# Three chained blocks on one core: the remainders of a float64 MoE moved from GpSimd to VectorE, and the second MoE's gathers, block order and scatters changed

## The chip, the cores and the metric

The kernel runs on one core of a Trainium2 chip. The metric is the device time of one execution in microseconds (us). The core has five engines with queues of their own: TensorE (PE in the profile; PEld is its weight load), VectorE (DVE), ScalarE (ACT), GpSimd (POOL) and SyncE (SP), which here only starts DMA transfers. Each engine runs its instructions in order; one that waits holds up all behind it on that engine.

## The reference, cut to what matters

```python
# attention: 4 batches, 12 heads, 448 rows, 64 wide; causal
scores = scale * q @ k^T;  scores = where(mask, -1e9, scores)
x = softmax(scores) @ v            # -> 1792 tokens x 768
# first MoE: every token through the same two matrices (float64 inputs)
h = x @ w_in                       # 768 -> 2048
x = (h - tanh(h)) @ w_out          # 2048 -> 768
# second MoE: one of 8 experts per token
logits = x @ w_gate + modality_bias[modality_id]
e = argmax(logits);  gate = softmax(logits)[e]
out[token] = gate * (relu(x[token] @ w1[e]) @ w2[e])   # 768 -> 1024 -> 768
```

`w_in` and `w_out` come as float64; the rest is float32.

## The kernel before

**Products in two parts.** Each float32 operand of a MoE product is split in two: `hi` is the value rounded to TensorE's fp32r format by a copy, and `lo` is the remainder, value minus `hi` (`split_lo`, line 69). A product is then three matmuls: hi x hi, hi x lo, lo x hi. `split_lo` takes the engine as an argument, and the copy before it has an engine of its own, so each split is a hand-over between two engines, or two instructions on one.

**Attention and the first MoE.** The tokens go in four batches of 448. While attention works on batch b+1 (six pairs of heads per batch, `attn_tick`), the first MoE works on batch b (`moe_steps`): 16 pieces of `w_in` in layer 1 (`l1`), 16 of `w_out` in layer 2 (`l2`), each piece 128 x 768. `take` hands out the MoE's steps between the attention's, in proportion to costs written in the list. `split_piece(n + 2)` is called as piece n is begun, so a piece is prepared two ahead; there are two buffers for `w_raw` and `w_lo` and three for `w_hi`. For batch 0 a piece is loaded as float64 words (`w_wide`, two buffers) and `narrow` (line 363) makes float32 of it: one conversion on ScalarE (L368), three integer instructions on VectorE (L372, L376, L380), and a DMA that keeps the narrowed piece in memory for batches 1 to 3. Then ScalarE copies `w_hi`, and GpSimd computes `w_lo` (line 396). GpSimd also computes `x_lo`, the remainder of attention's output, for all batches (line 406), and `g_lo`, the remainder between the two layers, for batch 0 (line 433); in later batches `g_lo` is on VectorE.

The softmax of batches 0 and 1 is left undivided, and the division is spread by small products (`ps_rc`, L273); in batches 2 and 3 VectorE divides.

**The second MoE.** Tokens are sorted by expert into blocks of 256 (`up_wide`) and one half block of 128 (`up_half`). The first two blocks (`first`) are of the expert that has most tokens after three batches, and are chosen before the fourth is through. `more()` routes the rest while block 0 runs, and returns five wide blocks, then the half block. A block needs 14 weight pieces: 6 of `w1` (128 x 1024) and 8 of `w2` (128 x 768), each fetched by an indirect DMA that GpSimd issues (`gather_w`), copied to `e_hi` on ScalarE and subtracted to `e_lo` on VectorE (`split_w`, line 910). There are four raw buffers (`e_raw`), and a gather is issued five pieces ahead of the one in work, a split two ahead. The first four gathers are issued while the first MoE still runs; splits 0 and 1 then go to a pool of their own (`e0`), and the pools `h` and `e` open only when the first MoE's memory is given back (`moe_ctx.close()`). Each block's rows are gathered by `gather_x` in the block before, and its results are scattered to `out` by an indirect DMA from GpSimd for each 128 rows (line 1090). All scatters write the same tensor, so each is ordered behind the one before.

**What sets the order.** The framework that the kernel is written in places the waits and buffers and sets each engine's order when the kernel is built, from the order of the program and its own modelled times; it may put an instruction that is ready before one that is not.

Of the kernel before, what the change touches and what calls it, by code (L numbers as in the profile page):

```python
# [8 lines left out]
F32 = mybir.dt.float32  # L9
# [8 lines left out]
P = 128  # L18
# [16 lines left out]
def kernel(  # L35
# [14 lines left out]
    nc = tc.nc  # L50
# [12 lines left out]
    def copy(eng, out, in_):  # L63
        if eng is nc.scalar:
            eng.activation(out=out, in_=in_, func=AF.Copy)  # L65
        else:
            eng.tensor_copy(out=out, in_=in_)

    def split_lo(eng, lo, full, hi):
        eng.tensor_tensor(out=lo, in0=full, in1=hi.bitcast(F32), op=ALU.subtract)  # L70
# [185 lines left out]
    def emit_pv(p):  # L256
# [26 lines left out]
        if b == 0:  # L283
            split_x(p)
        else:
            x_done.add(p)
# [31 lines left out]
    xhi, xlo = {}, {}  # L318
    pieces, raw_w = {}, {}
    NPC = 2 * KF  # L320
    order = [(b, j) for b in range(B) for j in range(NPC)]
# [3 lines left out]
    wide = w_in.dtype != F32  # L325
# [61 lines left out]
    def split_piece(n):  # L387
        if n >= len(order):
            return
        raw = raw_w.pop(n)  # L390
        if wide and order[n][0] == 0:
            raw = narrow(n, raw)
        hi = mp.tile([P, KD, P], F32R, tag="w_hi", name="w_hi", bufs=3)
        lo = mp.tile([P, KD, P], F32R, tag="w_lo", name="w_lo", bufs=2)
        copy(nc.scalar, hi, raw)
        split_lo(nc.gpsimd, lo, raw, hi)
        pieces[n] = (hi, lo)
        load_piece(n + 2)

    def split_x(p):  # L400
        b, hp = divmod(p, NP)
        xhi[b, hp] = mp.tile([P, S], F32R, tag=f"x_hi{hp}", name="x_hi")
        xlo[b, hp] = mp.tile([P, S], F32R, tag=f"x_lo{hp}", name="x_lo")
        t = x32.pop(p)
        copy(nc.scalar if b else nc.vector, xhi[b, hp], t)
        split_lo(nc.gpsimd, xlo[b, hp], t, xhi[b, hp])

    def moe_steps(b):
        base = b * NPC
        g_hi, g_lo = [], []  # L410
        cur = {}

        def l1(f, s):
            if s == 0:
                split_piece(base + f + 2)
                cur["ps"] = ps_m.tile([P, 512], F32, tag="m", name="ps_h")
            ps = cur["ps"][:, 0:S]
            whi, wlo = pieces[base + f]
            for kk in (2 * s, 2 * s + 1):
                for n, (a, x) in enumerate(((whi, xhi), (whi, xlo), (wlo, xhi))):  # L420
                    nc.tensor.matmul(  # L421
                        ps, a[:, kk, :], x[b, kk],
                        start=(kk == 0 and n == 0), stop=(kk == KD - 1 and n == 2),
                    )
            if s == 2:
                pieces.pop(base + f)
                t = mp.tile([P, S], F32, tag="tmp", name="tanh", bufs=2)
                nc.scalar.activation(out=t, in_=ps, func=AF.Tanh)  # L428
                nc.vector.tensor_tensor(out=t, in0=ps, in1=t, op=ALU.subtract)  # L429
                g_hi.append(mp.tile([P, S], F32R, tag=f"g_hi{f}", name="g_hi"))  # L430
                g_lo.append(mp.tile([P, S], F32R, tag=f"g_lo{f}", name="g_lo"))
                copy(nc.scalar if b == 0 else nc.vector, g_hi[f], t)
                split_lo(nc.gpsimd if b == 0 else nc.vector, g_lo[f], t, g_hi[f])

        def l2(j, s):
            if s == 0:
# [87 lines left out]
    pool2 = {}  # L524
    BT = 256
    NFIRST = 2
    NSTAT = NT // BT - NFIRST
    NBLK = (NT - 1 - (NT - S + E - 1) // E) // BT + E + 1
    FE = w1.shape[2]
# [64 lines left out]
    def ps_route(nm):  # L594
        if "r" in pool2:
            return pool2["r"].tile([P, 512], F32, tag="r", name=nm)
        return ps_t.tile([P, 512], F32, tag="t", name=nm)
# [288 lines left out]


    NT2 = BT // P
    G_AHEAD = 5
    w1r = w1.rearrange("e d f -> (e d) f")  # L890
    w2r = w2.rearrange("e f d -> (e f) d")

    def off(ap):
        return bass.IndirectOffsetOnAxis(ap=ap, axis=0)

    def gather_w(blk, i):
        t = pool2["w"].tile([P, FE], F32, tag="e_raw", name="e_raw", bufs=4)
        if i < KD:
            nc.gpsimd.indirect_dma_start(  # L899
                out=t, out_offset=None, in_=w1r, in_offset=off(blk["w1"][i]),  # L900
                bounds_check=E * DM - 1, oob_is_err=False,
            )
        else:
            nc.gpsimd.indirect_dma_start(
                out=t[:, 0:DM], out_offset=None, in_=w2r, in_offset=off(blk["w2"][i - KD]),
                bounds_check=E * FE - 1, oob_is_err=False,
            )
        blk["raw", i] = t
# [111 lines left out]
    def moe2(blocks, more=None):  # L1020
        seq = [(b, i) for b in blocks for i in range(KD + KE)]

        def ahead(n, f):
            if n < len(seq):
                f(*seq[n])

        if "xt" not in blocks[0]:
            gather_x(blocks[0])
            for n in range(G_AHEAD):
                ahead(n, gather_w)  # L1030
            for n in range(2):
                ahead(n, split_w)
            turn_x(blocks[0])
        else:
            ahead(G_AHEAD - 1, gather_w)
        for u, blk in enumerate(blocks):
            nxt = blocks[u + 1] if u + 1 < len(blocks) else None
            n0 = u * (KD + KE)
            nt = len(blk["g"])

            def step(i, n0=n0, nxt=nxt):
                ahead(n0 + i + 2, split_w)
                ahead(n0 + i + G_AHEAD, gather_w)
                if i == 2 and nxt is not None:
                    gather_x(nxt)

            hid = (up_wide if nt == NT2 else up_half)(blk, step)
            nch = DM // BT
            po = [
                pool2["l2"].tile([P, 2, BT], F32, tag=f"l2_{n}", name="ps_l2")  # L1050
                for n in range((nt * nch + 1) // 2)
            ]
            for f in range(KE):
                step(KD + f)
                whi, wlo = blk.pop(("w", KD + f))
                th, tl = hid[f]
                for t in range(nt):
                    ts_ = slice(t * P, (t + 1) * P)
                    for m, (a, w) in enumerate(((th, whi), (th, wlo), (tl, whi))):
                        for h in range(nch):  # L1060
                            c = t * nch + h
                            nc.tensor.matmul(  # L1062
                                po[c // 2][:, c % 2, :], a[:, ts_], w[:, h * BT:(h + 1) * BT],
                                start=(f == 0 and m == 0 and c % 2 == 0),
                                stop=(
                                    f == KE - 1 and m == 2
                                    and (c % 2 == 1 or c == nt * nch - 1)
                                ),
                            )
                if f == KE - 1 and u == 0 and more is not None:  # L1070
                    new = more()
                    blocks.extend(new)
                    seq.extend((b, i) for b in new for i in range(KD + KE))
                if f == KE - 3 and nxt is not None:
                    turn_x(nxt)
            for t in range(nt):
                ob = pool2["h"].tile([P, DM], F32, tag="ob", name="ob", bufs=4)
                gt = blk["x"][t][:, DM:DM + 1]
                h = 0
                while h < nch:  # L1080
                    c = t * nch + h
                    n = 2 if c % 2 == 0 and h + 1 < nch else 1
                    o = ob[:, h * BT:(h + n) * BT]
                    src = po[c // 2][:, c % 2:c % 2 + n, :].rearrange("p a b -> p (a b)")
                    if n == 2:
                        nc.scalar.activation(out=o, in_=src, func=AF.Copy, scale=gt)
                    else:
                        nc.vector.tensor_scalar_mul(o, src, gt)
                    h += n
                nc.gpsimd.indirect_dma_start(  # L1090
                    out=out, out_offset=off(blk["s"][t]), in_=ob, in_offset=None,
                    bounds_check=NT - 1, oob_is_err=False,
                )

    def clear_last():
        z = mp.tile([P, 768], F32, tag="w_raw", name="zrow", bufs=2)
# [8 lines left out]
    def run():  # L1105
# [66 lines left out]
            take(state["used"] + 0.1)  # L1172
        first = route_first(ps_route("ps_a"))
        gather_x(first[0])
        for i in range(4):
            gather_w(first[0], i)
        while len(state["fill"]) > 12:
            take(state["used"] + 0.1)
# [13 lines left out]
        routed = {}  # L1192

        def more():
            half, routed["rest"], routed["tot"] = route_rest(ps_route("ps_b"))
            return routed["rest"][:NSTAT] + [half]

        moe2(first, more)
        rest, tot = routed["rest"], routed["tot"]
        n = nc.values_load(tot[0:1, 0:1], min_val=0, max_val=NBLK)  # L1200
# [37 lines left out]
```

## Time and profile before

| | |
|---|---|
| three runs | 1057.69, 1058.78, 1059.7 us (median 1058.78) |
| profiled execution | 1053.05 us |
| its span, first to last instruction | 1051.3 us |
| mean granted clock of TensorE | 0.981 |
| TensorE busy, 0 to 89 us (attention of batch 0) | 79.7 |
| TensorE busy, 464 to 630 us (batch 2 of the first MoE) | 165.7 |
| TensorE busy, 630 to 766 us (batch 3, without attention beside it) | 131.2 |
| TensorE busy, 766 to 1051.3 us (second MoE) | 267.0 |

The profile is that of one execution. Its rows give an engine, a line of the kernel, output and inputs by name, how often, how long, and what ended the idle time before. The granted clock is the share of full speed that TensorE was given. Names are those of the program without buffer numbers.

### The profile page before, as it was taken

The page shows a single profiled execution, that of the slowest core. Times are in us where ns is not written, and L with a number is a line of the kernel's source. Part 1 is how long each engine was busy: PE and PEld are TensorE (multiplying, and loading weights), DVE is VectorE, ACT ScalarE, POOL GpSimd, SP SyncE. Part 2 cuts the span into 40 slices and gives each one's busy share as a digit, 9 for nine tenths or more (in the row PEclk, how much of TensorE's full clock was granted, in tenths as well). Part 3 has the DMA queues.
Part 4 walks back from the last instruction along what each step waited for, and adds up shares of the span by engine and source line. Part 5 has one row for each costly group of instructions (what it writes and reads, how often), then busy time and mean ns, then how long its engine had stood idle before and what let it go on. Part 6 is the DMA issues. An engine that isn't in the chain of part 4 may idle for free.

```text
span 1051.3 us, 17253 instructions
## 1 busy us (share of the span) xinstructions
PE 995.7 (95%) x6366; PEld 847.3 (81%) x6366; DVE 625.9 (60%) x1333; ACT 513.2 (49%) x1061; POOL 457.9 (44%) x326
## 2 busy tenths in 40 slices
PE   6999889698999999999999998999989999999994
PEld 3667667577777888878878887999889999999994
DVE  4867888757665663455674429641376645655563
ACT  4766556555554554444455433432234544554553
POOL 0215455333333443433353346554255465546552
PEclk9999999899999999999999999999989999999997
DMA  7744667676534344343323236343246676676763
GB/s 158 194 120 117 194 192 218 195 206 205 148 93 145 105 111 118 101 116 102 102 85 93 84 113 189 113 140 116 72 152 212 212 226 224 199 233 220 226 198 116
DMA packets 141564, 162.02 MB, mean 154 GB/s; under 512 B 77215, under 2 KB 112543, under 8 KB 141472
## 3 DMA queue, kind: packets, MB, share of 16 engines
q1 hardware_dynamic: 127040, 99.03, 33.5%
q0 software_dynamic: 14432, 61.81, 18.8%
q8 instruction: 52, 0.85, 0.3%
q14 instruction: 40, 0.33, 0.1%
HBM read 135.77 MB, written 25.43 MB: 153 GB/s over the span
## 4 chain that ended last, share of the span: by engine, by line
PE 67%; issue 9%; DVE 8%; POOL 6%; DMA 5%; ACT 4%; SPq 0%; POOLq 0%; ACTq 0%; DVEq 0%
PE ps_x L445 19%; PE ps_h L421 16%; PE ps_l L1062 8%; PE ps_sc L185 5%; PE ps_l L969 5%; PE ps_xt L262 4%; PE ps_pt L242 4%; DVE w_raw L376 2%; DVE w_raw L380 2%; POOL w_lo L70 2%; DMA e_raw<-in_moe_w_dram,a_i 2%; DMA e_raw<-in_moe_w_dram,b_i 1%; PE ps_tr L145 1%; ACT w_raw L368 1%; POOL e_raw L899 1%
## 5 line engine op out<-in xcount | busy, mean ns | idle before, releaser
L70 POOL TENSOR_TENSOR w_lo<-w_raw,w_hi 128x768 fp32r<-128x768 f32 x128 | 247.6, 1935 | 307.8 <-PE ps_x L445 124.3
L65 ACT ACTIVATE w_hi<-w_raw 128x768 fp32r<-128x768 f32 x128 | 107.9, 844 | 180.3 <-DMA w_raw<-w 115.9
L70 DVE TENSOR_TENSOR e_lo<-e_raw,e_hi 128x768 fp32r<-128x768 f32 (+1 forms) x112 | 119.7, 1072 | 111.3 <-ACT e_hi L916 110.8
L916 ACT ACTIVATE e_hi<-e_raw 128x768 fp32r<-128x768 f32 (+1 forms) x112 | 104.8, 939 | 137.6 <-PE ps_l L1062 59.6
L421 PE MATMUL ps_h<-x_hi,w_hi 128*128 128x448 f32 x384 | 151.9, 396 | 10.2 <-DVE tanh L429 10.1
L445 PE MATMUL ps_x<-g_hi,w_hi 128*128 128x448 f32 x384 | 150.8, 393 | 0.0
L421 PE MATMUL ps_h<-x_lo,w_hi 128*128 128x448 f32 x384 | 142.2, 370 | 1.2 <-POOL x_lo L70 1.2
L445 PE MATMUL ps_x<-g_hi,w_lo 128*128 128x448 f32 x384 | 141.7, 369 | 1.2 <-POOL w_lo L70 1.2
L421 PE MATMUL ps_h<-x_hi,w_lo 128*128 128x448 f32 x384 | 142.0, 370 | 0.5 <-POOL w_lo L70 0.5
L445 PE MATMUL ps_x<-g_lo,w_hi 128*128 128x448 f32 x384 | 141.8, 369 | 0.0
L211 ACT ACTIVATE s_sb<-s_sb,mx 112x112 f32<-112x112 f32 (+1 forms) x192 | 99.6, 521 | 76.5 <-DVE mx L195 76.1
L195 DVE CUSTOM_DVE_ANT_0 s_sb<-ps_sc,mask 112x112 f32<-112x112 f32 (+1 forms) x192 | 77.1, 443 | 67.2 <-PE ps_sc L185 66.5
L421 PEld LDWEIGHTS ps_h<-x_hi,w_hi 128*128 128x128 f32 x384 | 72.9, 190 | 31.0 <-DVE tanh L429 13.1
L969 PE MATMUL ps_l<-xt_hi,e_lo 128*128 128x256 f32 x336 | 94.4, 281 | 0.0
L969 PE MATMUL ps_l<-xt_hi,e_hi 128*128 128x256 f32 x336 | 94.1, 280 | 0.0
L969 PE MATMUL ps_l<-xt_lo,e_hi 128*128 128x256 f32 x336 | 93.6, 279 | 0.0
L445 PEld LDWEIGHTS ps_x<-g_hi,w_hi 128*128 128x128 f32 x384 | 73.2, 190 | 13.5 <-issue 7.9
L445 PEld LDWEIGHTS ps_x<-g_hi,w_lo 128*128 128x128 f32 x384 | 73.1, 190 | 7.9 <-POOL w_lo L70 1.9
L421 PEld LDWEIGHTS ps_h<-x_hi,w_lo 128*128 128x128 f32 x384 | 73.0, 190 | 6.9 <-POOL w_lo L70 0.9
L421 PEld LDWEIGHTS ps_h<-x_lo,w_hi 128*128 128x128 f32 x384 | 73.3, 191 | 6.1 <-POOL x_lo L70 1.8
L445 PEld LDWEIGHTS ps_x<-g_lo,w_hi 128*128 128x128 f32 x384 | 73.5, 191 | 4.4
L429 DVE TENSOR_TENSOR tanh<-ps_h,tanh 128x448 f32<-128x448 f32 x64 | 39.6, 619 | 60.2 <-ACT tanh L428 60.1
(216 smaller groups left out, 1934.5 us busy)
## 6 DMA issues: line engine op xcount, KB each, us to landing
w_raw<-w SPq DMA_DIRECT2D x96, 384.0 KB, 3.1
w_wide<-in_moe_w_in_dram SPq DMA_DIRECT2D x16, 768.0 KB, 5.6
w<-w_raw SPq DMA_DIRECT2D x32, 384.0 KB, 2.8
w_wide<-in_moe_w_out_dram SPq DMA_DIRECT2D x12, 768.0 KB, 4.9
qr<-in_q_dram SPq DMA_DIRECT2D x48, 112.0 KB, 3.2
kr<-in_k_dram SPq DMA_DIRECT2D x48, 112.0 KB, 3.2
vr<-in_v_dram SPq DMA_DIRECT2D x48, 112.0 KB, 3.2
x2s<-tok SPq DMA_DIRECT2D x24, 224.0 KB, 3.3
```

The source lines that it names most:

```text
L65: eng.activation(out=out, in_=in_, func=AF.Copy)
L70: eng.tensor_tensor(out=lo, in0=full, in1=hi.bitcast(F32), op=ALU.subtract)
L185: nc.tensor.matmul(ps[:CP, x, o:o + w], qT[r, c * CP:(c + 1) * CP], kT[r, 0:w], start=(o == 0), stop=(c == S_GROUPS[g][-1]),)
L195: nc.vector.tensor_tensor_reduce(out=d["s"][c], in0=ps[:CP, x, at[c]:at[c] + w], in1=mask[:, S - w:S], scale=1.0, scalar=3.0e38, op0=ALU.a ...
L211: nc.scalar.activation(out=s, in_=s, func=AF.Exp, scale=-1.0, bias=d["mx"][c], accum_out=sums[p][:, x, c:c + 1],)
L242: nc.tensor.transpose(ps[:CP, o + (c - kc) * CP:o + (c - kc + 1) * CP], d["s"][c][:, kc * CP:(kc + 1) * CP], ident[:CP, :CP],)
L262: nc.tensor.matmul(ps[64 * x:64 * x + 64, kc * CP:S], vt[:, kc, x, :], st[2 * p + x]["pt"][kc], start=(kc == 0), stop=(kc == NC - 1),)
L421: nc.tensor.matmul(ps, a[:, kk, :], x[b, kk], start=(kk == 0 and n == 0), stop=(kk == KD - 1 and n == 2),)
L445: nc.tensor.matmul(ps, a[:, r, :], x[f], start=(f == 0 and n == 0), stop=(f == KF - 1 and n == 2),)
L916: nc.scalar.activation(out=hi[:, 0:n], in_=raw[:, 0:n], func=AF.Copy)
L969: nc.tensor.matmul(o, a[:, fs], x, start=(kk == 0 and m == 0 and f % 2 == 0), stop=(kk == KD - 1 and m == 2 and f % 2 == 1),)
L1062: nc.tensor.matmul(po[c // 2][:, c % 2, :], a[:, ts_], w[:, h * BT:(h + 1) * BT], start=(f == 0 and m == 0 and c % 2 == 0), stop=(f == KE ...
```

## The change

1. The remainders of the first MoE that were on GpSimd in batch 0 go to VectorE: `w_lo` of the 32 pieces that are narrowed, `x_lo` of batches 0 and 1 (12 of 24), and `g_lo` of batch 0 (16).
2. The second MoE's gathers have eight raw buffers: four as before and four in pool `e`, used in turn by fours. A gather is issued nine pieces ahead. Before the second MoE still only the first four are issued; pieces 4 to 8 follow at its start.
3. The half block comes third, ahead of the five wide blocks of the rest.
4. The scatters to `out` are declared independent of each other, since no two write the same row.

```diff
@@ split_piece
-        split_lo(nc.gpsimd, lo, raw, hi)
+        split_lo(nc.vector if wide and order[n][0] == 0 else nc.gpsimd, lo, raw, hi)
@@ split_x
-        split_lo(nc.gpsimd, xlo[b, hp], t, xhi[b, hp])
+        split_lo(nc.vector if b < 2 else nc.gpsimd, xlo[b, hp], t, xhi[b, hp])
@@ l1
-                split_lo(nc.gpsimd if b == 0 else nc.vector, g_lo[f], t, g_hi[f])
+                split_lo(nc.vector, g_lo[f], t, g_hi[f])
@@ second MoE
-    G_AHEAD = 5
+    G_FIRST = 4
+    G_LATE = 4
+    G_AHEAD = G_FIRST + G_LATE + 1
+    gathered = [0]
@@ gather_w
-        t = pool2["w"].tile([P, FE], F32, tag="e_raw", name="e_raw", bufs=4)
+        late = gathered[0] % (G_FIRST + G_LATE) >= G_FIRST
+        gathered[0] += 1
+        t = pool2["e" if late else "w"].tile(
+            [P, FE], F32, tag="e_raw", name="e_raw", bufs=G_LATE if late else G_FIRST
+        )
@@ moe2
-            ahead(G_AHEAD - 1, gather_w)
+            for n in range(G_FIRST, G_AHEAD):
+                ahead(n, gather_w)
@@ scatter
-                nc.gpsimd.indirect_dma_start(
+                put = nc.gpsimd.indirect_dma_start(
                     out=out, out_offset=off(blk["s"][t]), in_=ob, in_offset=None,
                     bounds_check=NT - 1, oob_is_err=False,
                 )
+                tc.declare_no_dep(put.ins, group="rows_of_out", reason="disjoint rows")
+                tc.add_to_no_dep_group("rows_of_out", put.ins)
@@ more
-            return routed["rest"][:NSTAT] + [half]
+            return [half] + routed["rest"][:NSTAT]
```

## Rows read from the trace of the kernel before

**Rows 1.** The page: busy time by engine; the chain that ended last.

```profile
PE 995.7 (95%) x6366; PEld 847.3 (81%) x6366; DVE 625.9 (60%) x1333; ACT 513.2 (49%) x1061; POOL 457.9 (44%) x326
PE 67%; issue 9%; DVE 8%; POOL 6%; DMA 5%; ACT 4%; SPq 0%; POOLq 0%; ACTq 0%; DVEq 0%
```

**Rows 2.** Table by stage: stretch, length, busy us per engine, PEclk, DMA, GB/s.

```profile
89.00:185.00 96.00, 85.08 (x486) 67.53 (x482) 81.08 (x116) 56.00 (x126) 53.15 (x32) 0.96 0.65 191
185.00:292.00 107.00, 95.31 (x552) 75.38 (x552) 71.88 (x140) 56.12 (x128) 38.68 (x22) 0.94 0.64 187
292.00:372.00 80.00, 80.00 (x456) 64.31 (x456) 51.42 (x135) 40.62 (x100) 30.69 (x18) 1.00 0.41 116
372.00:464.00 92.00, 91.66 (x527) 73.73 (x525) 44.18 (x121) 46.02 (x113) 36.09 (x21) 1.00 0.42 113
```

**Rows 3.** Groups, whole span: xcount | busy us, mean ns | idle before, releaser.

```profile
L70 DVE TENSOR_TENSOR e_lo<-e_raw,e_hi 128x768 fp32r<-128x768 f32 x64 | 61.2, 957 | 71.3 <-ACT e_hi L916 71.1
L70 DVE TENSOR_TENSOR g_lo<-tanh,g_hi 128x448 fp32r<-128x448 f32 x48 | 33.0, 687 | 1.3
L273 PE MATMUL ps_rc<-ident,sm 112*64 112x112 f32 x192 | 13.9, 261 | 0.0
```

**Rows 4.** The chain of waits, 89 to 212: start us, us, what.

```profile
101.06 0.95 ACT w_raw L368
102.71 2.48 DVE w_raw L376
107.53 0.81 ACT w_raw L368
```

**Rows 5.** The narrowing on VectorE: count, duration min/median/max in ns, starts.

```profile
L372 DVE TENSOR_SCALAR w_raw<-w_raw x32: 542/561/1748, 25.1 to 272.4; 128x768 int32<-128x768 int32 x32
L376 DVE SCALAR_TENSOR_TENSOR w_raw<-w_wide,w_raw x32: 943/959/2477, 25.7 to 273.5; 128x768 int32<-128x768 int32 x32
L380 DVE SCALAR_TENSOR_TENSOR w_raw<-w_wide,w_raw x32: 941/958/2482, 28.8 to 274.9; 128x768 int32<-128x768 int32 x32
```

**Rows 6.** GpSimd's timeline, 85 to 130: start us, us, instruction.

```profile
102.22 2.15 POOL L70 TENSOR_TENSOR w_lo<-w_raw,w_hi 128x768 fp32r<-128x768 f32 x1
```

**Rows 7.** Groups of instructions on VectorE, 89 to 185.

```profile
L380 DVE SCALAR_TENSOR_TENSOR w_raw<-w_wide,w_raw 128x768 int32<-128x768 int32 x15 | 24.2, 1611 | 0.3
L376 DVE SCALAR_TENSOR_TENSOR w_raw<-w_wide,w_raw 128x768 int32<-128x768 int32 x15 | 24.0, 1599 | 0.4
L372 DVE TENSOR_SCALAR w_raw<-w_raw 128x768 int32<-128x768 int32 x15 | 11.9, 792 | 11.5 <-ACT w_raw L368 11.5
```

**Rows 8.** Groups of instructions on VectorE, 185 to 292.

```profile
L380 DVE SCALAR_TENSOR_TENSOR w_raw<-w_wide,w_raw 128x768 int32<-128x768 int32 x13 | 16.8, 1289 | 0.2
L376 DVE SCALAR_TENSOR_TENSOR w_raw<-w_wide,w_raw 128x768 int32<-128x768 int32 x13 | 13.3, 1026 | 0.3
```

**Rows 9.** Groups of instructions on ScalarE, 185 to 292.

```profile
L368 ACT ACTIVATE w_raw<-w_wide 128x768 f32<-128x768 f32 x13 | 11.7, 897 | 10.2 <-POOL w_lo L70 10.2
```

**Rows 10.** Table of two stretches at the start of the second MoE.

```profile
776.00:780.00 4.00, 1.82 (x16) 1.61 (x14) 2.88 (x17) 1.06 (x2) 2.36 (x4) 1.00 0.93 304
780.00:788.00 8.00, 6.84 (x35) 6.80 (x36) 7.49 (x23) 4.14 (x7) 3.68 (x4) 0.57 0.61 190
```

**Rows 11.** The gathers of w2 (line 904): durations in ns, and time to landing.

```profile
L904 POOL DMA_INDIRECT e_raw<-in_moe_w_dram,a_i x16: 995/999/4191, 766.2 to 822.0; - x16
DMA to landing us min/median/max: 3.6/4.4/7.0
```

**Rows 12.** GpSimd's timeline, 758 to 800.

```profile
766.21 4.19 POOL L904 DMA_INDIRECT e_raw<-in_moe_w_dram,a_i  x1 [13.76 <-DVE rank L670]
```

**Rows 13.** The chain of waits, whole span: one wide block's first layer.

```profile
911.20 16.97 PE ps_l L969 x144
```

**Rows 14.** VectorE's timeline, 758 to 782.

```profile
765.95 3.48 DVE L70 TENSOR_TENSOR e_lo<-e_raw,e_hi 128x1024 fp32r<-128x1024 f32 x3
```

**Rows 15.** Table of the half block's stretch at the end.

```profile
1017.40:1041.10 23.70, 19.94 (x118) 17.48 (x116) 13.61 (x16) 12.44 (x17) 12.87 (x10) 0.93 0.59 187
```

More of the change, by code (lines that the diff above doesn't have):

```diff
@@ L1174, in run @@
         gather_x(first[0])
-        for i in range(4):
+        for i in range(G_FIRST):
             gather_w(first[0], i)
```

## The prediction

> **What bounds the kernel now.** I read the page first. TensorE is busy 95% of the span and is most of the chain that ended last, but 8% of that chain is VectorE and 6% GpSimd [rows 1]. So the whole gain to be had is the 5% in which TensorE stands still, plus what its clock loses there. The table by stage says where that is. Batch 0 of the first MoE (the one that narrows the float64 weights) takes 96.0 us for its first layer and 107.0 us for its second; batch 1, which does the same products from weights already narrowed, takes 80.0 and 92.0 us [rows 2]. TensorE stands 10.9 and 11.7 us idle in the two stretches of batch 0, and its mean granted clock is 0.96 and 0.94 there, against 1.00 later. Of the 31 us between the batches some is real work: the plain softmax of batches 0 and 1 has `ps_rc` products, 13.9 us over 12 pairs [rows 3], so 1.16 us each and some 3.5 us per stretch. TensorE's floor is thus about 83.5 us for layer 1 and 95.2 us (91.7 busy in batch 1, and 3.5) for layer 2.
>
> The chain shows why batch 0 is slower. It runs in a ring between ScalarE and VectorE: ScalarE's conversion L368, VectorE's L372, L376, L380, then ScalarE's `w_hi` copy and the next L368. One turn, from 101.06 to 107.53, takes 6.47 us for one piece, and 2.48 of it is a single L376 [rows 4]. The same instruction takes 0.94 us at best and 0.96 in the median, and L380 the same [rows 5]. The long one began at 102.71, while GpSimd's `w_lo` ran from 102.22 to 104.37 [rows 6], and ended 0.82 us after it: nearly its whole own time lay after GpSimd was done. In layer 1 the means are 1.61 and 1.60 us [rows 7]. GpSimd's subtraction holds up the engine that the chain goes through.
>
> **The change, part by part.** Every sum is made against the profiled execution, 1053.05 us (span 1051.3 and 1.75 around it), which lies 5.73 us under the median of the three runs, 1058.78; I carry that difference over unchanged.
>
> *Remainders, layer 1 (89 to 185).* VectorE is busy 81.1 us. Its 15 narrowings cost 24.2 + 24.0 + 11.9 = 60.1 us [rows 7]; at the medians 0.561 + 0.959 + 0.958 [rows 5] it is 15 x 2.48 = 37.2, so 22.9 us come free. Added: 15 `w_lo` at 0.957, the price of the same subtraction of 128x768 in the second MoE; 15 `g_lo` at 0.687; some 3 `x_lo` of the same shape at 0.687 [rows 3]: 14.4 + 10.3 + 2.1 = 26.8. VectorE then has 85.0 us of work, just over TensorE's floor. It has to wait besides, since each `w_lo` follows a ScalarE copy of the same piece, and each `g_lo` one of `g_hi`; queued behind them on VectorE are the next narrowing, the next `tanh` subtraction and the attention's row maxima, for which ScalarE and TensorE wait. The `e_lo` rows give the far bound of such a wait, 71.1 us over 64, 1.11 us each; the near bound is nothing, when other work stands between the two. The order on each engine is set when the kernel is built, by modelled times that put ready work into such a gap, and the stretch has other VectorE work to put there; so I take 0.3 us each, nearer to the low end: 30 x 0.3 = 9. Layer 1 comes to 94, a gain of 2 us, between +11 (85.0, no wait) and the loss of the rival below.
>
> *Remainders, layer 2 (185 to 292).* L380 and L376 cost 16.8 + 13.3 over 13 pieces [rows 8]; at the medians 24.9, so 5.2 free. Added: 13 `w_lo`, 12.4, and 4 `x_lo`, 2.7. VectorE's 71.9 us become 81.8, well under TensorE's 95.2. What goes is the wait of ScalarE's L368 for `w_lo`, 10.2 us [rows 9], since GpSimd's subtraction, over 2 us long [rows 6], and its queue no longer hold the two `w_raw` buffers. Late next is TensorE itself. I take its floor and 2 us: 97, a gain of 10 us, between 3 (only the 5.2 us of VectorE, less half for its new waits) and 11.8.
>
> *The six `x_lo` of batch 0* fall before 89: 4.1 us more on VectorE, hidden under TensorE's attention. I take nothing; uncovered it is 4.1.
>
> *Eight raw buffers, nine gathers ahead.* At the start of the second MoE TensorE runs out. Of 776 to 788 it is idle 2.18 + 1.16 = 3.3 us, and for the 6.84 us in which it then works the granted clock is 0.57, mostly the lower of its two levels (1.2, not 2.4 GHz), after that idling: about 2.9 us more [rows 10]. The cause is in the gathers: the first of `w2` began only at 766.2 and took 4.19 us to issue [rows 12], where the median takes 1.0, and a piece lands 4.4 us after its issue, 7.0 at the latest [rows 11], because all four raw buffers were full until the splits that need the second MoE's own buffers could run. With four more buffers five gathers go out as soon as the first MoE's memory is free. But two of them, pieces 4 and 5, used to be fetched long before, into the first buffers. TensorE takes 16.97 / 6 = 2.83 us per piece of `w1` [rows 13], and ends the six at about 777.8, so it wants piece 4 at about 772. Issued at 764 (my choice, two us before that gather, as the splits began before it) and landed 5 us later at 769, copied and subtracted in about 2.4 us (three `e_lo` of 128x1024 take 3.48 [rows 14], so 1.16 each, and I take the copy as long), it is there at 771.4: just in time. I take 5 of the 6.2 us. If the gather goes out only at 766.2 and lands 5.5 us later (between the two landing times), piece 4 is there at 774.1: TensorE stops for 2 us, the clock may dip again, and the step loses 2.
>
> The Trainium skill (SBUF — State Buffer, "Who interferes with whom") has a rule that matters here: VectorE's two-port modes starve GpSimd's descriptor writing, while a subtraction of two SBUF tensors does not (it says the latter is inferred). The trace seems to speak against the second half: the issue of 4.19 us began at 766.2, beside the three `e_lo` subtractions, back to back from 765.95 on [rows 12, 14]. By the page all five late gathers issue at 1.0 us and the term is 6.2; by the row each that meets `e_lo` may be slow, and it is the loss of 2.
>
> *Half block third, free scatters.* Now the half block is last and takes 23.7 us, of which TensorE works 19.9 [rows 15]; from its end at 1041.1 another 10.2 us pass to the end of the span. Third, it draws its 14 pieces from buffers that are ahead, and most of the 3.8 us idle goes: 2.5. The end gets a second scatter behind a wide block, 1.3 us (an issue of 1.0 and a gap). Net gain 1.2, from -3 (the half is starved there as well and the next block too) to +3. The freed order of the scatters pays only in that the second doesn't wait for the first to land, some 4.4 us; elsewhere gathers stand between the two, nothing.
>
> Sum: 2 + 10 + 5 + 1.2 = 18.2. 1053.05 - 18.2 = 1034.85, and with 5.73 the median is 1040.6 us.
>
> **The rivals.**
> *VectorE becomes the bound of layer 1 (slower).* Each of the 30 new waits there costs the full 1.11 us of the `e_lo` rows: 33 us, so layer 1 takes 85.0 + 33 = 118, 22 longer. Layer 2 has 81.8 + 14.4 = 96.2 of VectorE, still about TensorE's floor, and gains its 10; the second MoE gains 6.2. Net 6 us slower: 1064.6. It decides where layer 1 passes 112 us, at 0.9 us per wait. For it: VectorE at 85 of 96 with two new hand-overs per piece. Against: in the second MoE VectorE has little else to do while it waits; here it has.
>
> *The ring stays.* The 1.5 us that L376 gives back in a turn are taken by `w_lo` (0.957) and the copy before it, because L372 of the next piece is queued behind them. Layer 1 gains nothing, layer 2 only 4, the second MoE 6.2: 1048.6. For it: the 6.47 us turn has no slack beside its own steps. Against: `w_lo` can run while ScalarE does the next L368 (0.95).
>
> *Late pieces 4 and 5*, or slow issues: the second MoE's start loses 2 instead of gaining 5: 1047.6.
>
> That the change doesn't do what it says can't be here: the trace shows the narrowing itself (L368 to L380), so the weights are float64 and the conditions hold for 32 pieces.
>
> **How the numbers follow.** Forecast 0.61, the ring 0.20, late pieces 0.10, VectorE 0.09. The forecast's best is 1058.78 - (11 + 11.8 + 6.2 + 3) = 1026.8. The range goes from 1027 to 1056: it takes in the ring and the late pieces, and both together (1055.6), and leaves out the slower case. A measurement here tells 0.2% (2.1 us) from no change. Faster takes the forecast, ring and late pieces, less 0.05 for two mishaps at once: 0.86; slower 0.08, the rest of the slower case and of those mishaps within 0.2%: 0.06.
>
> **What would show it.** In the changed profile L376 and L380 should have means near 0.96 in layer 1, and GpSimd no arithmetic before batch 1's first pieces. Layer 1 near 94 and layer 2 near 97 us, with granted clock near 1.00, show the first two terms; a VectorE wait of `w_lo` for `w_hi` of 1 us each, or layer 1 over 112, shows the rival. At the second MoE's start TensorE should run through the change from up to down without the 0.57 clock; a wait for `e_raw` of `w1` shows pieces 4 and 5 late. The half block should take about 21 us. The prediction is wrong if batch 0 still takes 203 us although L376 has got short.

## The result and the profile after

The changed kernel takes 1028.06 us (median of four runs, 1024.04 to 1031.06); the kernel before took 1058.63 beside it. The ratio is 0.9706, 95% interval 0.9676 to 0.9737: 31 us faster, where 18.2 were forecast (1040.6, range 1027 to 1056). The sign, the range and the mechanism hold; most sizes do not.

The profiled execution took 1024.04 us, its span 1022.0. From its page: busy time, then the chain that ended last, by engine.

```profile
PE 985.8 (96%) x6366; PEld 839.3 (82%) x6366; DVE 628.9 (62%) x1393; ACT 515.2 (50%) x1061; POOL 363.2 (36%) x266
...
PE 76%; DVE 7%; DMA 5%; issue 5%; ACT 4%; POOL 1%; SPq 1%; POOLq 0%; ACTq 0%; DVEq 0%
```

Against [rows 1], TensorE's share of the chain went from 67 to 76%, and GpSimd's from 6 to 1%.

To see where the time came from, I read off TensorE's timeline when certain products start, as fixed stretches shift when the work in them gets faster:

| start of | before | after | gained so far |
|---|---|---|---|
| batch 0, layer 1, third piece | 90.9 | 89.1 | 1.8 |
| batch 0, layer 2 | 180.0 | 165.1 | 14.9 |
| batch 1, layer 1 (after the last product of batch 0) | 289.5 | 259.4 | 30.1 |
| second MoE, first wide block | 759.8 | 730.6 | 29.2 |
| end of the span | 1051.3 | 1022.0 | 29.3 |

In these two profiles all of it comes in batch 0: 15 us by the end of its first layer, 15 in its second. The table by stage, columns as in [rows 2]; below the dots, the start of the second MoE and the half block:

```profile
89.00:165.00 76.00, 75.17 (x456) 60.25 (x455) 72.85 (x136) 54.43 (x123) 0.00 (x0) 1.00 0.77 224
...
262.00:342.00 80.00, 80.00 (x454) 64.31 (x453) 49.76 (x135) 40.79 (x100) 30.78 (x18) 1.00 0.40 116
...
748.00:752.00 4.00, 2.72 (x24) 2.52 (x23) 4.00 (x10) 2.29 (x5) 3.39 (x3) 1.00 0.64 190
803.80:827.60 23.80, 21.25 (x132) 19.04 (x131) 17.07 (x21) 16.88 (x23) 18.45 (x15) 0.93 0.76 248
```

Layer 1 of batch 0 now runs with TensorE 99% and VectorE 96% busy, GpSimd not at all, and the clock at its full level. Here are VectorE's instructions in that stretch (count, busy us, mean ns, idle before), to be held against [rows 7]:

```profile
L70 DVE TENSOR_TENSOR w_lo<-w_raw,w_hi 128x768 fp32r<-128x768 f32 x14 | 13.4, 955 | 0.7 <-ACT w_hi L65 0.6
L376 DVE SCALAR_TENSOR_TENSOR w_raw<-w_wide,w_raw 128x768 int32<-128x768 int32 x14 | 13.4, 954 | 0.2
L380 DVE SCALAR_TENSOR_TENSOR w_raw<-w_wide,w_raw 128x768 int32<-128x768 int32 x14 | 13.3, 953 | 0.1
L70 DVE TENSOR_TENSOR g_lo<-tanh,g_hi 128x448 fp32r<-128x448 f32 x15 | 9.3, 618 | 0.3 <-ACT g_hi L65 0.2
...
L372 DVE TENSOR_SCALAR w_raw<-w_raw 128x768 int32<-128x768 int32 x13 | 7.2, 556 | 1.7 <-ACT w_raw L368 1.7
```

L376 and L380 are at 0.95 us, from 1.60 and 1.61. The new subtractions wait 0.7 us over 14 and 0.3 over 15, and VectorE's wait for L368 is down from 11.5 to 1.7 us.

### The profile page after: what moved, and what is told of

The parts are those of the page before. It is cut to its first block, busy times and chain, and to the rows that moved or that the text cites. A ratio compares the mean times of both kernels' runs of the same rounds, so it can differ in the third digit from the quotient of the medians.

```text
span 1022.0 us, 17235 instructions
## 1 busy us (share of the span) xinstructions
PE 985.8 (96%) x6366; PEld 839.3 (82%) x6366; DVE 628.9 (62%) x1393; ACT 515.2 (50%) x1061; POOL 363.2 (36%) x266
## 4 chain that ended last, share of the span: by engine, by line
PE 76%; DVE 7%; DMA 5%; issue 5%; ACT 4%; POOL 1%; SPq 1%; POOLq 0%; ACTq 0%; DVEq 0%
PE ps_x L445 21%; PE ps_h L421 17%; PE ps_l L1070 11%; PE ps_l L976 9%; PE ps_sc L185 5%; PE ps_xt L262 4%; PE ps_pt L242 4%; DMA w_wide<-in_moe_w_in_dram 2%; DMA w_wide<-in_moe_w_out_dram 2%; PE ps_tr L145 1%; PE ps_xg L951 1%; ACT w_raw L368 1%; DVE w_raw L376 1%; PE ps_x2t L467 1%; DVE w_raw L380 1%
## 5 line engine op out<-in xcount | busy, mean ns | idle before, releaser
L70 POOL TENSOR_TENSOR w_lo<-w_raw,w_hi 128x768 fp32r<-128x768 f32 x96 | 179.3, 1869 | 494.1 <-PE ps_x L445 341.6
L211 ACT ACTIVATE s_sb<-s_sb,mx 112x112 f32<-112x112 f32 (+2 forms) x192 | 99.6, 521 | 69.4 <-DVE mx L195 69.0
L429 DVE TENSOR_TENSOR tanh<-ps_h,tanh 128x448 f32<-128x448 f32 x64 | 39.7, 620 | 56.8 <-ACT tanh L428 56.6
```

The source lines that it names most:

```text
L211: nc.scalar.activation(out=s, in_=s, func=AF.Exp, scale=-1.0, bias=d["mx"][c], accum_out=sums[p][:, x, c:c + 1],)
```

## The experiments

They went in four groups, each on one chip beside the kernel before, whose median was 1057.35, 1058.44, 1052.94 and 1059.15 us; so kernels of different groups are compared by their ratios.

| kernel | group | median us | ratio | 95% |
|---|---|---|---|---|
| changed kernel | | 1028.06 | 0.9706 | 0.9676 to 0.9737 |
| first MoE's edits alone | 1 | 1028.72 | 0.9731 | 0.9701 to 0.9761 |
| the same, with a GpSimd subtraction that nobody reads | 1 | 1048.00 | 0.9913 | 0.9885 to 0.9942 |
| before, three `w_raw` and `w_lo` buffers | 1 | 1052.51 | 0.9951 | 0.9937 to 0.9964 |
| only `w_lo` moved | 1 | 1039.30 | 0.9840 | 0.9808 to 0.9872 |
| first MoE, eight raw buffers | 2 | 1021.17 | 0.9661 | 0.9638 to 0.9684 |
| first MoE, half third | 2 | 1034.04 | 0.9774 | 0.9752 to 0.9795 |
| first MoE, eight raw buffers, free scatters | 2 | 1022.99 | 0.9673 | 0.9655 to 0.9690 |
| second MoE's edits alone | 2 | 1055.30 | 0.9970 | 0.9956 to 0.9984 |
| first MoE, eight raw buffers, relu ahead | 3 | 1016.22 | 0.9666 | 0.9643 to 0.9689 |
| changed kernel, rows gathered a block earlier | 3 | 1020.20 | 0.9678 | 0.9656 to 0.9701 |
| first MoE, eight raw buffers, three `w_wide` | 3 | 1010.25 | 0.9595 | 0.9580 to 0.9611 |
| the same, relu ahead | 4 | 1012.53 | 0.9572 | 0.9546 to 0.9598 |

**First MoE alone, second MoE alone.** The first three hunks of the change, and the rest of it.

> Only the edits of the first MoE (32 w_lo, 12 x_lo, 16 g_lo on VectorE); gathers, block order and scatters as before. Theory A (the whole gain is in batch 0, the second MoE's edits add up to about nothing): 1028, between 1025 and 1031, with the events of batch 0 as in the changed kernel (first product of layer 2 near 165 us, batch 1 near 262) and the second MoE as before (285 us, with the low clock at its start). Theory B (the second MoE's edits are worth the forecast 6): 1034.

> Only the second MoE's edits (buffers, half third, free scatters), the first MoE as before. If the parts add up: the changed kernel less the first MoE's edits alone, 1057.35 - 0.7 = 1056.7, between 1055 and 1059. If the second MoE's edits are worth the forecast 6.2: 1051.

0.9731 and 0.9970. The parts add up (their product is 0.9702; the whole gave 0.9706): 28.6 us from the first MoE, 3.1 from the second. Theory B falls. Theory A holds for batch 0: in the first run layer 2 starts at 166.0 and batch 1 at 260.2. The second MoE's edits are little, but not nothing: their interval ends at 0.9984, and in the first run the second MoE took 294.5 us from its first wide block to the end, where the profile before has 291.5 (more on this below).

**A subtraction that nobody reads.** The kernel of the first MoE's edits, with this after each `split_lo` of the 32 pieces (the scratch tile `sh` holds zeros):

```diff
+            nc.gpsimd.tensor_copy(out=sh[:, 0, 0:1], in_=lo[:, 0, 0:1].bitcast(F32))
+            nc.gpsimd.tensor_tensor(out=sh, in0=sh, in1=sh, op=ALU.subtract)
```

> As the run before, and for each of the 32 narrowed pieces GpSimd subtracts a scratch tile of 128x768 from itself, started by the finished w_lo, with no reader. Theory A (GpSimd's arithmetic holds up VectorE's instructions that run beside it, whoever needs its result): L376 and L380 go back to means of 1.4 to 1.7 us in layer 1, VectorE, 96% busy there without it, becomes the bound, and at least half of the 30 us is lost: 1043 to 1060. Rival C (the gain is that nobody waits for GpSimd's slower result any more): L376 and L380 stay at 0.96 and the time at 1028 to 1030.

1048.0: 19.3 of the 28.6 us are lost, to a result that is never used; in its trace no instruction waits for it. Rival C falls as the main cause. Layer 1 ends 10.7 us later (176.7). VectorE's groups in it, first without the subtraction (89 to 166), then with it (89 to 176.7):

```profile
L376 DVE SCALAR_TENSOR_TENSOR w_raw<-w_wide,w_raw 128x768 int32<-128x768 int32 x14 | 13.3, 954 | 0.2
L380 DVE SCALAR_TENSOR_TENSOR w_raw<-w_wide,w_raw 128x768 int32<-128x768 int32 x14 | 13.3, 952 | 0.1
L429 DVE TENSOR_TENSOR tanh<-ps_h,tanh 128x448 f32<-128x448 f32 x14 | 8.6, 616 | 0.1
L372 DVE TENSOR_SCALAR w_raw<-w_raw 128x768 int32<-128x768 int32 x14 | 7.8, 554 | 1.4 <-ACT w_raw L368 1.2
```

```profile
L376 DVE SCALAR_TENSOR_TENSOR w_raw<-w_wide,w_raw 128x768 int32<-128x768 int32 x14 | 15.6, 1113 | 0.2
L380 DVE SCALAR_TENSOR_TENSOR w_raw<-w_wide,w_raw 128x768 int32<-128x768 int32 x13 | 15.1, 1162 | 0.1
...
L372 DVE TENSOR_SCALAR w_raw<-w_raw 128x768 int32<-128x768 int32 x14 | 12.8, 916 | 1.6 <-ACT w_raw L368 1.6
...
L441 DVE TENSOR_TENSOR tanh<-ps_h,tanh 128x448 f32<-128x448 f32 x14 | 8.6, 614 | 0.1
```

The narrowing got 14 x 0.159 + 13 x 0.210 + 14 x 0.362 = 10.0 us longer, nearly the whole delay; the `tanh` subtraction, which reads one operand from PSUM (where the `ps_` tiles lie), did not (L441 here is L429 there). The means rose less than expected (1.1, not 1.4 to 1.7), as the subtraction comes right after `w_lo`, where it often meets L372. One case, GpSimd's timeline and then VectorE's of this kernel, from 100 to 112:

```profile
104.16 1.85 POOL L408 TENSOR_TENSOR shadow<-shadow 128x768 f32<-128x768 f32 x1
```

```profile
104.60 0.62 DVE L279 TENSOR_TENSOR x<-ps_xt,x 128x448 f32<-128x448 f32 x1
105.13 1.69 DVE L376 SCALAR_TENSOR_TENSOR w_raw<-w_wide,w_raw 128x768 int32<-128x768 int32 x1
```

GpSimd runs to 106.01. L279, with one operand in PSUM, takes its usual 0.62 meanwhile; L376, with both in SBUF (where the tiles of other names lie), ends 0.81 after GpSimd and has taken 0.74 too long, as in [rows 4, 6].

The kernel before shows the same without an experiment, if its 32 narrowings are parted by whether a subtraction of GpSimd ran beside them (by start and duration of both). L376: 16 alone, none over 0.96 us; 16 beside one, 1.62 in the mean. L380: 16 alone, none over 0.96; 16 beside, 1.84. L372: 20 alone, none over 0.57; 12 beside, 1.02.

The other 9.3 of the 28.6 us are not parted by this run. GpSimd's unread subtractions were 23.8 us in layer 1, where its work before was 50.8, so some of the 9.3 may be the same cause, and some the hand-over.

**More buffers instead.** The kernel before with `bufs=3` for the tags `w_raw` and `w_lo`.

> The kernel before with three buffers for w_raw and w_lo in place of two, all remainders on GpSimd. Rival C (GpSimd's late result holds the buffers, and that is what costs): ScalarE's conversion no longer waits for w_lo, and most of the 30 us is gained: 1030 to 1042. Theory A (VectorE is held up during GpSimd's arithmetic): L376 and L380 keep their means of 1.6 us in layer 1, layer 1 keeps its 91 us, only layer 2 gains, up to 8 us: 1050 to 1058.

1052.5: a gain of 4.8 us. L380 kept its 1.64 us in layer 1, L376 came down to 1.24 and L372 went up to 0.90: 3.8 us a piece, where it was 4.0, and the layer still ended at 178.3. So most of the 30 us was not held by the buffers. The third buffer took away only a part of the hand-over, though: L368 still waited 7.6 us for `w_lo` in the two layers, from 11.7.

**Only `w_lo`.** The first hunk alone.

> Only the 32 w_lo go to VectorE; x_lo and g_lo stay on GpSimd. Theory A by amount of GpSimd work: in layer 1 GpSimd keeps the g_lo, about 19 of its 51 us, so L376 and L380 fall to about 1.2 us, not 0.96, and about two thirds of the gain is there: 1034 to 1041. Rival C: w_lo alone held buffers, so the whole gain: 1028 to 1030.

1039.3, a gain of 18 of 28.6 us, with L376 at 1.16 and L380 at 1.18 in layer 1 while GpSimd still did 14 `g_lo` (19.4 us): as theory A had it, the loss goes with the amount of GpSimd's work.

**The second MoE's edits one by one**, each on the first MoE's: buffers (hunks of `G_FIRST` to `gather_w` and `moe2`), the order in `more()`, and buffers with the free scatters.

> The first MoE's edits and the eight raw buffers with nine gathers ahead; half block last, scatters ordered as before. The run with the first MoE's edits alone gave 1028.7. Both theories: 5 us gained at the start of the second MoE (no low clock there). Theory D (the 1.1 us that each later wide block takes longer in the changed kernel comes from the deeper gathers): five blocks give 5.5 back, 1028 to 1030. Theory E (it comes from the half block standing third): 1022 to 1025, with wide blocks 35.7 us apart.

> The first MoE's edits and the half block third; four raw buffers, five gathers ahead, scatters ordered. Theory D: wide blocks 35.7 us apart as before, the half block no shorter (23 to 24 us, its rows' gathers stand behind the scatters in GpSimd's queue), the end 1 to 2 us longer with its two scatters: 1029 to 1031. Theory E: five wide blocks at 36.8: 1034 to 1036.

> The run with first MoE and buffers, and the scatters declared independent, half block last. Expected the same time within 1 us of that run, as the gathers between two scatters take longer than the first takes to land. If a scatter's wait does hold up the gathers of the next block (both are in GpSimd's queue): 2 to 5 us faster than that run, in the wide blocks.

The buffers gain (0.9661 over 0.9731: 0.7%, 7.6 us). The half block third loses: 0.9774 over 0.9731 is 4.7 us, and on eight buffers the changed kernel over the one with buffers and free scatters is 0.3%. In both pairs the intervals overlap; the traces, from the first wide block to the end, say the same: 299.2 against 294.5 us, and 291.4 against 288.3. Free scatters alone change nothing. Neither D nor E was right in its reason: the wide blocks took 36.9 us in all three, and in the run of the first MoE's edits too, where the second MoE is the one before. The 37 us are no work of the change; more below. What differs most is the half block. The stretch of it at the end, with four buffers (first MoE's edits alone) and with eight:

```profile
991.10:1015.40 24.30, 19.99 (x118) 17.38 (x116) 13.58 (x16) 12.48 (x17) 12.48 (x10) 0.93 0.55 180
```

```profile
989.50:1009.50 20.00, 18.86 (x118) 16.19 (x116) 13.44 (x16) 12.43 (x17) 8.10 (x6) 1.00 0.41 134
```

Eight buffers alone take it from 24.3 to 20.0 us and its clock from 0.93 to 1.00, where it stands last. Third, with the same buffers, it takes 23.8 (the profile after, above). With four buffers it takes 24.9 in the third place, little more than the 24.3 at the end; there the loss is at the end of the kernel, where 14.5 us pass after TensorE's last product, from 10.8: two ordered scatters stand behind the last wide block.

**Rows gathered a block earlier.** The changed kernel with this:

```diff
-            xg = pool2["w"].tile([P, XW], F32, tag="xg", name="xg", bufs=2 * NT2)
+            xg = pool2["w"].tile([P, XW], F32, tag="xg", name="xg", bufs=3 * NT2)
...
-                if i == 2 and nxt is not None:
+                if i == 2 and nxt is not None and "x" not in nxt:
                     gather_x(nxt)
...
+                if f == KE - 1 and u + 2 < len(blocks):
+                    gather_x(blocks[u + 2])
```

> The changed kernel, with each block's rows gathered a block earlier, ahead of the scatters (six xg buffers in place of four). Theory F (the half block third takes 23.7 us and not 20 because the rows of the next block are gathered behind two scatters in GpSimd's queue): half block 20 to 21 us, 1023 to 1026 in all. Rival G (it is the weight pieces, or a half block third is too short for the 14 pieces of the wide block behind it): half block 23 to 24, 1027 to 1029.

0.9678 against 0.9706, 3 us, though the two intervals overlap and the chips differ. The trace decides for theory F. GpSimd's timeline of the changed kernel in the half block (the row of `xg` is the gather of the next block's rows):

```profile
804.40 1.00 POOL L911 DMA_INDIRECT e_raw<-in_moe_w_dram,b_i  x1 [1.81 <-DVE e_lo L70]
805.70 2.06 POOL L1098 DMA_INDIRECT out_dram<-ob,a_ids  x1 [0.30 <-issue]
808.07 1.94 POOL L1098 DMA_INDIRECT out_dram<-ob,a_ids  x1 [0.30 <-ACT e_hi L923]
810.31 1.05 POOL L911 DMA_INDIRECT e_raw<-in_moe_w_dram,b_i  x1 [0.30 <-DVE e_lo L70]
811.67 1.01 POOL L931 DMA_INDIRECT xg<-x2s,b_idg  x1 [0.31 <-issue]
```

and what TensorE and its weight load waited for at the turning of those rows (L951), from 800 to 830:

```profile
  DMA xg<-x2s,b_idg: 4.4, 2
```

That is one wait, counted for each of the two: TensorE stood 2.1 us, and then had 4 us (816 to 820) at a granted clock of 0.58, which costs another 1.7. With the rows gathered earlier that wait is gone, and the half block has this stretch:

```profile
809.80:830.00 20.20, 19.73 (x130) 17.42 (x129) 16.83 (x21) 16.88 (x22) 16.00 (x12) 1.00 0.72 234
```

**Relu ahead.** ScalarE's queue has `e_hi` of a piece of `w2` ahead of the four `h_hi` that begin the second half of a wide block. On the kernel with first MoE and buffers:

```diff
-            nc.scalar.activation(out=th, in_=ps[g], func=AF.Relu)
+            blk["relu"] = nc.scalar.activation(out=th, in_=ps[g], func=AF.Relu).ins
...
-                step(KD + f)
+                if f == 0 and nt == NT2:
+                    with tc.issue_after(blk["relu"]):
+                        step(KD + f)
+                else:
+                    step(KD + f)
```

> As the run with first MoE and buffers (half block last), and in each wide block ScalarE's e_hi of the third piece of w2, which stands ahead of the four relu copies h_hi in its queue and waits there for a weight buffer, is queued behind them. Theory E2 (that wait is what makes most wide blocks 36.9 us long and not 35.7): wide blocks 35.7 us or less, four to six times 1.2 us: 1014 to 1017. Rival E3 (the products themselves are reported late to ScalarE, so h_hi waits just as long; the e_hi copy, 0.85 us, is the only thing gained or is paid again behind it): 1019 to 1022.

0.9666, no gain over 0.9661, but inconclusive: on this chip the wide blocks took 35.5 us in the kernel without this edit too (the next one), so there was nothing to mend.

**Three `w_wide` buffers.** On the kernel with first MoE and buffers, `bufs=3` for `w_wide`.

> As the run with first MoE and buffers, and three w_wide buffers in place of two, so that the float64 pieces are fetched earlier. Theory H (after the change the loads of w_wide are what is late next in batch 0: the chain goes through six of them, ScalarE's conversion waits 6 us for them): 2 to 4 us faster than 1021.2. Rival I (TensorE is 99% busy in layer 1 already, there is nothing left): 1020 to 1022.

0.9595 over 0.9661, 7 us: theory H, and more than it expected. Batch 0's two layers, before this edit and with it:

```profile
89.00:165.70 76.70, 75.96 (x464) 61.24 (x462) 73.85 (x139) 55.42 (x126) 0.00 (x0) 1.00 0.76 223
165.70:261.60 95.90, 93.43 (x563) 73.96 (x561) 80.24 (x159) 56.23 (x124) 3.31 (x2) 1.00 0.73 219
```

```profile
89.00:164.00 75.00, 75.00 (x461) 60.73 (x458) 73.29 (x141) 56.64 (x127) 0.00 (x0) 1.00 0.77 231
164.00:255.70 91.70, 91.44 (x562) 73.95 (x561) 80.11 (x159) 55.27 (x124) 3.38 (x2) 1.00 0.73 218
```

Together 5.9 us, 4.2 of them in layer 2, where TensorE no longer stands still. The rest of the 7 is within the two intervals; on the same chip, against the kernel with relu ahead, it was 6.0 (1010.25 and 1016.22).

**Both.** `bufs=3` for `w_wide` and the relu ahead.

> The two last edits together on the first MoE's edits and the buffers, half block last: three w_wide buffers, and e_hi of the third piece of w2 queued behind the relu copies. Ratio to the kernel before 0.9595 if the relu order is worth nothing (so it was where the wide blocks took 35.5 us anyway). If this execution shows the long seam (36.9 us per wide block in the runs with first MoE's edits alone and with the buffers): by theory E2 the wide blocks still take 35.5 here and the ratio is 0.953 to 0.956; by rival E3 they take 36.0 to 36.9 and the ratio is 0.958 to 0.960.

0.9572, between the two forecasts; its interval holds the 0.9595 of the kernel without the relu order. Here the seam was slow again and the wide blocks took 36.0 us: the `e_hi` copy is saved, the rest is not. It is a version 4.3% faster than before, against 2.9% of the change; whether the relu order adds to `w_wide` isn't settled.

## Why the prediction came out as it did

**Right: the mechanism.** The long L376 and L380 were held up by GpSimd's arithmetic; they went to 0.95 us, and the run with an unread subtraction shows it as the main cause. The Trainium skill (SBUF — State Buffer, "Who interferes with whom") says that a VectorE instruction with two SBUF inputs contends with a GpSimd instruction that reads SBUF, over a pair of ports that it calls an exclusive lock, while a VectorE instruction with at most one SBUF input and outside the two-port modes does not contend. The 1.69 us of L376 and the 0.62 of L279 agree. L372 has one SBUF input and was held, 0.92 us for 0.55; the same section of the Trainium skill counts `tensor_scalar`, which it is, among those that can enter such a mode. Which mode it ran in no run here shows.

**Mis-sized: layer 1, forecast 2, measured 13 to 15.** Two terms failed. "VectorE then has 85.0 us of work" and "TensorE's floor is thus about 83.5" were sums over 89 to 185, a stretch with bounds read from the clock. By its products, layer 1 ended at 180.0 there, and of its 16 pieces two had been all but multiplied by 89. The 80.0 us of batch 1 were for over 15 of its 16 pieces (by products it ran from 289.5 to 372.9). For the 14 left TensorE was busy for 75.2 us and VectorE for 72.9, as the table by stage shows. VectorE's sum was too high in other places too: the stretch took in 4.0 us of layer 2 (VectorE was busy 77.1 from 89 to 180) and three `x_lo` that belong to it, and adding up durations counts twice where the records of neighbouring instructions overlap. The instructions that begin in layer 1 add up to 82.6 us before and 82.4 after, so what came free paid for what was added. And "0.3 us each" for the new waits, 9 us, was 1.0 over 29, 0.03 each: there was nearly always other work between the copy and the subtraction. `g_lo`, priced at 0.687 after the mean of the whole span, took 0.618; that mean held two of over 2.1 us that began beside a `w_lo` of GpSimd.

**Mis-sized: layer 2, forecast 10, measured 15.** The same fault: by its products it ran from 180.0 to 289.5, 109.5 us, and takes 94.3 now. "I take its floor and 2 us: 97" counted 95.2 as TensorE's floor; with three `w_wide` buffers the whole layer takes 91.7. The 91.7 of batch 1 that the floor was made from were read from 372 to 464, and its layer 2 ran from 372.9 to 461.8, 88.9 us; with the 3.5 of `ps_rc` that is 92.4. So the gain went past the bound of 11.8 that I had put on it. What is late next is not TensorE, as I wrote, but the loads of `w_wide`, for which ScalarE's L368 waits 9.7 us in the two layers after the change:

```profile
L368 ACT ACTIVATE w_raw<-w_wide 128x768 f32<-128x768 f32 x27 | 24.5, 907 | 14.2 <-DMA w_wide<-in_moe_w_out_dram 6.2 <-DMA w_wide<-in_moe_w_in_dram 3.5 <-DVE w_lo L70 1.2
```

**Not nothing: what falls before 89.** The six `x_lo` of batch 0 were taken at nothing. The third piece starts 1.8 us earlier after the change (0.9 between the run with only `w_lo` moved, 90.8, and that with all edits of the first MoE, 89.9). Which of the moved remainders gives it no run tells.

**Less than forecast: the start of the second MoE, forecast 5, measured 1 to 4.** In the profile after the clock stays at 1.00 where it was 0.57 [rows 10], and the first wide block takes 38.4 us, from 41.2 in the run of the first MoE's edits: 2.8, and 1 to 4 between the other pairs of profiles. The steady clock was in part luck. TensorE still stands at that place, 1.3 us in the profile after, for VectorE's `h_lo` (L986); and of the eight profiles with eight buffers four kept 1.00 there, while in four the clock fell to between 0.65 and 0.73 in the 4 us behind the stop (0.73 in the one with free scatters and the half block last, whose first wide block takes 40.3 us). The late pieces were not late: five gathers began between 734.5 and 740.5, and took 1.0 to 1.8 us to issue.

**Wrong: the half block.** "Third, it draws its 14 pieces from buffers that are ahead, and most of the 3.8 us idle goes": it is the buffers that do this, wherever the block stands, and third it loses it again to the rows of the next block, queued behind two scatters. The end got longer by 1.7 us, 12.2 after TensorE's last product from 10.5 with the half block last (the term had 1.3). My bound of -3 had the half starved in the third place as well, and so it was, only for those rows and not for weights. "The freed order of the scatters" was worth what it undid: with the half third and ordered scatters the second waits 3.4 us at the end (forecast 4.4):

```profile
1018.91 1.01 POOL L1090 DMA_INDIRECT out_dram<-ob,b_ids  x1 [15.34 <-ACT ob L1086]
1023.33 0.99 POOL L1090 DMA_INDIRECT out_dram<-ob,b_ids  x1 [3.41 <-DMA out_dram<-ob,b_ids]
```

**A gap I carried over without asking.** The profiled execution of before lay 5.73 us under the median of its runs. Its later wide blocks were 35.5 to 35.8 us apart but for one, those of the first MoE's edits, with the same second MoE, 36.9 or 37.0 but for one. So the two profiles, before and after, put the second MoE at 291.5 and 291.4 us, and hide the 3 us that its edits are worth in timed runs. The groups fit this: the kernel before took 1052.94 us on the chip of group 3, whose traces all have the short distance, and 1057.35 to 1059.15 on the others. The profile after has the long distance and lies 4.0 us under its own median all the same, so this is not the whole of such gaps.

**The rivals.** VectorE as the bound needed 0.9 us per wait: it was 0.03. The ring needed L372 of the next piece to queue behind `w_lo` and lose 1.5 us: VectorE's wait for L368 fell to 1.7 us over 13.

## What to carry to other kernels

Before moving work between engines, ask whether the two hold each other up: compare an instruction's time alone with its time beside the other engine's work. An engine off the path can hold up one on it until its own instruction is done (L376 above, 2.48 us for 0.96), and a copy of the work that nobody reads, left on the old engine, separates most of that from the hand-over in one run. Size a stage by its first and last product, not by the clock of the old profile, since floors from another batch hold only for the same pieces, and look at more than one profile before a clock that held is put down to the change. A reordering that rests on a resource (here the raw buffers) should be tried after the resource alone; here the buffers had the gain, and the order took about half of it back in the traces.

## What was unexpected of the hardware

*Issues beside `e_lo`.* Of the DMAs that GpSimd issued in the changed kernel, 69 had over 0.3 us of an `e_lo` beside their issue, by start and duration of both; 28 of these took over 1.2 us. Of the 73 others one did. The Trainium skill (SBUF — State Buffer, "Who interferes with whom") reports that `tensor_tensor` did not stall DMA in a probe, with a reason that it marks as inferred; these numbers, like the 4.19 us of [rows 12], speak against that. The price here was some 1 us for most scatters. By which way the two meet no run here shows.

*A seam that differs between executions.* In the traces of the changed kernel and of groups 1 and 2 ScalarE starts the `e_hi` ahead of `h_hi` some 16.5 us after most wide blocks begin, and these blocks take 36.9 us; in those of group 3 that have the same order it is 14.2 to 14.4, and the blocks take 35.5 or 35.6. ScalarE's timeline with the long seam, in the kernel of first MoE's edits (the block began at 882.3):

```profile
893.75 0.85 ACT L916 ACTIVATE e_hi<-e_raw 128x768 fp32r<-128x768 f32 x1 [2.00 <-PE ps_l L969]
898.85 0.85 ACT L916 ACTIVATE e_hi<-e_raw 128x768 fp32r<-128x768 f32 x1 [4.25 <-PE ps_l L969]
899.60 1.55 ACT L978 ACTIVATE h_hi<-ps_l 128x512 fp32r<-128x512 f32 x3
```

The buffer that it waits for was last read by products that TensorE's timeline ends 2 us earlier: 5 x 2.83 after 882.3 is 896.5. So TensorE's completion seems to reach ScalarE 2 us late, once in most wide blocks, in groups 1, 2 and 4 and not in group 3. It is not the buffer alone: with relu ahead, in group 4 (block at 912.4), `h_hi` waits for no such buffer and still starts only 16.7 us after the block began, where it is 15.0 with the same order in group 3:

```profile
929.14 2.07 ACT L985 ACTIVATE h_hi<-ps_l 128x512 fp32r<-128x512 f32 x4 [4.36 <-PE ps_l L976]
```

What delays it is open; no run here was made to tell.
